# Retention attention ahead of two MLPs on one Trainium2 core: another order of the attention output rows, and the first weight matrix fetched in that order

## The chip, the cores and the metric

The kernel runs on one core of one Trainium2 chip. The metric is the device time of one execution, in microseconds (us), lower is better. The engines of the core are named as in the profile: PE (matmuls), PEld (the loads of a matmul's stationary operand, which overlap PE), DVE, ACT, POOL (element-wise engines) and SP, which here only issues DMAs.

## The reference

What is computed, cut to its core (float32 throughout):

```python
def _attn_ref(q, k, v):            # each (2, 8, 768, 64): batch, heads, tokens, head size
    gamma = 1.0 - 2.0 ** (-5.0 - np.arange(H))          # a decay for each head
    for t in range(S):
        state = gamma[None, :, None, None] * state + einsum('bhd,bhe->bhde', k[:, :, t], v[:, :, t])
        y[:, :, t] = scale * einsum('bhd,bhde->bhe', q[:, :, t], state)

x = attn.transpose(0, 2, 1, 3).reshape(1536, 512)       # feature = head * 64 + e
x = (softplus(x @ moe_w_in)) @ moe_w_out                # 512 -> 2048 -> 512
out = (h * clip(h + 3, 0, 6) / 6) @ moe2_w_out          # h = x @ moe2_w_in, 512 -> 2048 -> 512
```

The weights come as 64-bit floats; the kernel takes them apart itself.

## The kernel before

**Units.** The recurrence is computed in 12 units (2 batches of 6 chunks of 128 tokens), `attend(u)`. A unit has five blocks of matmuls on PE: transposes of k and q (`Tk`, `Tq`), `scores` (S: k against q), `product` (D: k against v, the new state), `carry` (C: the old state against q) and `inner` (I: the masked scores against v). Apart from the transposes, all operands are 64 by 64, a quarter of PE's array: the rows that a matmul uses are the partitions of its operands (0 to 63 or 64 to 127), the columns are the partitions of its output. So there are four **quadrants**, and the program speaks of them through `part[0]` and `part[1]`. A matmul of 64 by 64 in float32 is two MATMUL records in the trace; C, with 16 matmuls, has 32 records. D of a batch's last unit and C of a batch's first unit are half as long.

**Where heads lie.** Head h = 2p + g has its q, k and state on partitions `part[g]` of column block p. Before the change the output of head h is also put on `part[g]` of block p, so that row p * 128 + partition is feature h * 64 + e in the natural order. C therefore goes from rows `part[g]` to columns `part[g]` and uses two of the four quadrants, in turn (L468 to L473). I goes from rows `part[j]` (the two halves of the chunk) to columns `part[g]`, with j innermost, and comes by all four quadrants every two heads (L478 to L483). S and D (all but the short one) use all four in the same way.

**After the matmuls.** DVE makes `pt` from the scores (times the mask, L433); I waits for it. C's output is in one PSUM bank, `oc`; ACT copies it to `oe` (L504); I's output is in two banks, `oi`; DVE adds the two into `on` (L506), and ACT and DVE split that into `x_hi` and `x_lo`, the input of the first MLP.

**MLPs.** All 1536 tokens go in three chunks of 512 through `gemm1` (G1, one bank `h`) and `gemm2` (G2, four banks `acc`, held over 16 steps). Each is twelve matmuls of 128x128 by 128x512 a step. The weights are fetched by `weight(m, o, f)`: 32 pieces of 512 KB for each MLP (16 of the input matrix, o = 0, and 16 of the output matrix), into three slots `raw`, and taken apart by ACT and DVE in some six operations each; the slot is free again after the last of them that reads it. Piece f of an input matrix is one DMA of 128 partitions with four runs of 1 KB on each (L251).

**Order.** `Plan` is a list scheduler that runs while the program is built. Every piece of work is a task with an engine, a cost, a due time and the slots or banks it takes; for each engine the task that can start within a small margin (`NEAR`, 0.5 us on PE) of the earliest and is due first is put next. Due times of PE's tasks are the running sum of the table `cost` (L197). A wait that the plan thinks longer than the margin is filled with another task. `places` gives banks: for one key the bank that came free first, for two keys two **neighbouring** banks (L64 to L67). The first eight units have slots of their own (`hold`), the last four (u = 8 to 11, where tiles appear in the trace as `cv` and `raw`) live in slots that the first weights have left. On the chip each engine takes its instructions in the order of the plan.

Of the kernel before, what the change touches and what calls it, by code (L numbers as in the profile page):

```python
# [13 lines left out]
AF = mybir.ActivationFunctionType  # L14
ALU = mybir.AluOpType
PSUM = bass.MemoryType.PSUM
P = 128
HALF = P // 2
# [101 lines left out]
PSX, TT, TS, ACP, ACS = 0.61, 0.62, 0.36, 0.49, 0.55  # L120
GEMM = 2.73
# [3 lines left out]
def kernel(ctx, tc, q, k, v, w1_in, w1_out, w2_in, w2_out, tq, tk, tcc, out):  # L125
    nc = Plan(tc)
    B, H, S, D = q.shape
    NT, DM = out.shape
    DFF = w1_in.shape[1]
    NP = H // 2  # L130
    KD = DM // P
    NF = DFF // P
    C = P
# [24 lines left out]
    banks = pool("psum", PSUM).tile([P, 8, CH], F32, name="banks")  # L158
# [35 lines left out]


    G = [(m, c, f) for m in range(2) for c in range(NC) for f in range(NF)]
    cost = {"Tk": 0.46, "Tq": 0.46, "S": 0.60, "D": 0.60, "C": 0.98, "I": 0.60, "G1": GEMM, "G2": GEMM}  # L197
    pe = [("Tk", 0), ("Tq", 0)]
    for u in range(START):
        pe += [("S", u), ("D", u)] + ([("Tk", u + 1), ("Tq", u + 1)] if u + 1 < START else []) + [("C", u), ("I", u)]  # L200
# [9 lines left out]
    n = 0  # L210
# [6 lines left out]
    due, t = {}, 5.0  # L217
# [3 lines left out]
    T = {}  # L221
# [7 lines left out]
    def weight(m, o, f, number):  # L229
        key = m, o, f  # L230
        made = conv[0] if m == 0 else []
        use = due[("G2" if o else "G1"), min(m * NC * NF + f, len(G) - LAG)] - 4.0

        def raw():
            return at_slot((f"raw{m}", key))

        def low_word():
            return raw()[:, :, 0]

        def y():  # L240
            return raw()[:, :, 1]

        def w():
            return at_slot((f"cv{m}", key))

        def fetch():
            src = words[m][o]
            if o:
                nc.sync.dma_start(out=raw().rearrange("p n t -> p (n t)"), in_=src[f * P:(f + 1) * P, :])
            else:  # L250
                nc.sync.dma_start(out=raw().rearrange("p (k n) t -> p k (n t)", k=KD),  # L251
                                  in_=src[:, 2 * f * P:2 * (f + 1) * P].rearrange("(k p) f -> p k f", p=P))

        def scale():
            nc.scalar.activation(y().bitcast(F32), y().bitcast(F32), AF.Copy, scale=2.0 ** -112)

        def bits():
            nc.scalar.activation(w(), low_word(), AF.Relu, scale=2.0 ** -29 * (1 - 2.0 ** -12), bias=half)

        def clamp():  # L260
            nc.vector.tensor_scalar(y().bitcast(F32), y().bitcast(F32), -TOP, TOP, ALU.max, ALU.min)

        def sign():
            nc.vector.scalar_tensor_tensor(w(), y(), 0x80000000, w(), ALU.bitwise_and, ALU.bitwise_or)

        def shift():
            nc.vector.scalar_tensor_tensor(w(), y(), 3, w(), ALU.logical_shift_left, ALU.bitwise_or)

        def shifted():
            nc.vector.tensor_scalar(w(), y(), 3, None, ALU.logical_shift_left)  # L270

        def merge():
            nc.vector.scalar_tensor_tensor(w(), low_word(), 29, w(), ALU.logical_shift_right, ALU.bitwise_or)

        def high():
            nc.scalar.activation(w_part(key, 0), w().bitcast(F32), AF.Copy)

        def negative():
            nc.scalar.activation(w_part(key, 1), w().bitcast(F32), AF.Copy, scale=-1.0)

        def low():
            nc.vector.tensor_tensor(w_part(key, 1), w().bitcast(F32), w_part(key, 0).bitcast(F32), ALU.subtract)

        def add():
            nc.gpsimd.dma_start(out=w_part(key, 1).bitcast(F32), in_=w().bitcast(F32), accum_op=ALU.add)

        raw_k, cv_k = (f"raw{m}", key), (f"cv{m}", key)
        cv, part = [(f"cv{m}", cv_k)], [("w", ("w", key))]
        tail = 1.5 if BY_DVE(number) else 7.0
        T["F", key] = t0 = nc.add("SP", 0.45, fetch, due=use - tail - 8.0, take=[(f"raw{m}", raw_k)], load=1.45 if o else 1.75)  # L290
        t1 = nc.add("ACT", 0.57, scale, [t0], use - tail - 3.5)
        t3 = nc.add("DVE", TS, clamp, [t1], use - tail - 2.5)
        if BITS(number):
            t2 = nc.add("ACT", 0.65, bits, [t0], use - tail - 3.0, take=cv)
            t4 = nc.add("DVE", TT, sign, [t3, t2], use - tail - 2.0)
            t5 = nc.add("DVE", TT, shift, [t4], use - tail - 1.3, give=[raw_k])
        else:
            t4 = nc.add("DVE", TS, shifted, [t3], use - tail - 2.4, take=cv)
            t4 = nc.add("DVE", TT, sign, [t4], use - tail - 2.0)
            t5 = nc.add("DVE", TT, merge, [t4], use - tail - 1.3, give=[raw_k])  # L300
        if BY_DVE(number):
            a = nc.add("ACT", ACS, high, [t5], use - 1.5, take=part, give=[cv_k] + made)
            b = nc.add("DVE", TT, low, [a], use - 0.7, give=[cv_k] + made)
        else:
            n = nc.add("ACT", ACS, negative, [t5], use - tail, take=part)
            b = nc.add("POOL", 0.9, add, [n], use - tail + 1, give=[cv_k] + made, load=1.6)
            a = nc.add("ACT", ACS, high, [n], use - 2.5, give=[cv_k] + made)
        T["W", key] = [a, b]
# [49 lines left out]
    def sub(keys, j):  # L358
        i = sorted(nc.slot[x][1] for x in keys)[j]
        return banks[:, i, :NP * HALF].rearrange("p (n t) -> p n t", n=NP)  # L360

    def bank(key):
        return at_slot(key).rearrange("p (n t) -> p n t", n=NP)

    part = [slice(j * HALF, (j + 1) * HALF) for j in range(2)]
    tables, ready = {}, {}

    def attend(u):
        b, i = divmod(u, NCH)
        ph = int(u >= FIRST)  # L370
        d = {n: due.get((n, u)) for n in cost}
        first, last = i == 0, i == NCH - 1
        mine = second if ph else arena

        def task(eng, cost, fn, after, when, take=(), give=(), load=0.0):
            return nc.add(eng, cost, fn, after, when, [(p, k) for p, k in take], list(give) + mine, load)

        def tile_of(n):
            return at_slot((n, u))
# [28 lines left out]
        def turned(n):  # L408
            def go():
                for p in range(NP):  # L410
# [5 lines left out]
                  take=own("kT"), give=[("kP", u)])  # L416
# [7 lines left out]
        sc, ds, oi = ([(n, j, u) for j in range(2)] for n in ("sc", "ds", "oi"))  # L424
# [32 lines left out]
        if not last:  # L457
# [7 lines left out]
            e = task("DVE", 0.42, total, [sm], d["C"] - 0.5, take=[end], give=ds + [mid[1]])  # L465
            ready["end", u] = task("DVE", 0.42, faded, [e, tables["c"]], due["C", u + 1] - 2.0, give=[end[1]])

        def carry():  # L468
            for j in range(int(first), 2):
                w = at_slot(mid[1] if j else ("end", u - 1))  # L470
                for p in range(NP):
                    for g in range(2):
                        nc.tensor.matmul(bank(("oc", u))[part[g], p, part[j]], w[part[g], p, :], tile_of("qT")[part[g], p, part[j]])  # L473

        c = task("PE", cost["C"] / (1 + first), carry, [qt, sm, None if first else ready["end", u - 1]], d["C"],
                 take=[("bank", ("oc", u))], give=[mid[1], ("qT", u)] + ([] if first else [("end", u - 1)]))

        def inner():  # L478
            for h in range(H):
                g, p = h % 2, h // 2  # L480
                for j in range(2):
                    nc.tensor.matmul(sub(oi, j)[part[g], p, :], tile_of("vs")[part[j], h, :], tile_of("pt").rearrange(
                        "p n (g t) -> p g n t", g=2)[part[j], g, p, :])  # L483

        n = task("PE", cost["I"], inner, [pt, vs], d["I"], take=[("bank", x) for x in oi], give=[("pt", u), ("vs", u)])
# [4 lines left out]
        def split(t):  # L490
            return t.rearrange("p n (j t) -> p j n t", j=2)

        def of(n):
            return at_slot((n, u)).rearrange("p (n t) -> p n t", n=NP)

        if first:
            o0 = task("ACT", 0.35, lambda: nc.scalar.activation(split(of("on"))[:, 0], sub(oi, 0), AF.Copy), [n], d["I"] + 0.7,
                      take=[("g", ("on", u))], give=oi)
            o1 = task("ACT", 0.35, lambda: nc.scalar.activation(split(of("oe"))[:, 1], split(bank(("oc", u)))[:, 1], AF.Copy), [c],
                      d["I"], take=[("e", ("oe", u))], give=[("oc", u)])  # L500
            on = task("DVE", 0.42, lambda: nc.vector.tensor_tensor(split(of("on"))[:, 1], split(of("oe"))[:, 1], sub(oi, 1), ALU.add),
                      [n, o0, o1], d["I"] + 1.0, give=oi + [("oe", u)])
        else:
            o1 = task("ACT", ACP, lambda: nc.scalar.activation(of("oe"), bank(("oc", u)), AF.Copy), [c],  # L504
                      d["I"], take=[("e", ("oe", u))], give=[("oc", u)])
            on = task("DVE", PSX, lambda: nc.vector.tensor_tensor(split(of("on")), split(of("oe")), both(oi), ALU.add),  # L506
                      [n, o1], d["I"] + 1.0, take=[("g", ("on", u))], give=oi + [("oe", u)])
        o2 = task("ACT", ACS, lambda: nc.scalar.activation(hi, of("on"), AF.Copy), [on], need - 1.5, give=[("on", u)])
# [147 lines left out]
```

## Time and profile before

| what | us |
|---|---|
| device time, median of 3 runs (607.19 to 609.77) | 607.47 |
| device time of the profiled execution | 606.65 |
| its span, first to last instruction | 604.5 |
| PE busy | 582.9 (96%) |
| DVE busy | 335.9 (56%) |
| ACT busy | 304.7 (50%) |

The span is 2.15 us shorter than the device time of the same execution. Busy shares are means over stages that differ: up to about 128 us the weights of the first MLP are fetched and taken apart, and DVE, ACT and the DMA queues are busier than the shares of the table say; from there on PE works almost without a gap. The mean granted clock of PE is 0.992 of full speed.

### The profile page before, as it was taken

The page shows a single profiled execution, that of the slowest core. Times are in us where ns is not written, and L with a number is a line of the kernel's source. Part 1 is how long each engine was busy: PE and PEld are TensorE (multiplying, and loading weights), DVE is VectorE, ACT ScalarE, POOL GpSimd, SP SyncE. Part 2 cuts the span into 40 slices and gives each one's busy share as a digit, 9 for nine tenths or more (in the row PEclk, how much of TensorE's full clock was granted, in tenths as well). Part 3 has the DMA queues.
Part 4 walks back from the last instruction along what each step waited for, and adds up shares of the span by engine and source line. Part 5 has one row for each costly group of instructions (what it writes and reads, how often), then busy time and mean ns, then how long its engine had stood idle before and what let it go on. Part 6 is the DMA issues. An engine that isn't in the chain of part 4 may idle for free.

```text
span 604.5 us, 9654 instructions
## 1 busy us (share of the span) xinstructions
PE 582.9 (96%) x3891; PEld 478.2 (79%) x3891; DVE 335.9 (56%) x584; ACT 304.7 (50%) x516; POOL 44.3 (7%) x57
## 2 busy tenths in 40 slices
PE   7698889999999999999999999999999999999997
PEld 6576668878788888888888887888888888888886
DVE  4899898995655333376677985622422222322223
ACT  2468877994533333476779996622222222222220
POOL 0001111120000000011122221100000000000000
PEclk9899989999999999999999999999999999999999
DMA  8997776966210100046588987510100000100001
GB/s 193 237 252 199 195 183 158 241 180 137 54 37 21 51 0 1 1 105 157 152 196 212 247 211 176 130 18 0 71 1 1 0 1 0 71 0 1 0 1 69
DMA packets 68364, 59.87 MB, mean 99 GB/s; under 512 B 39776, under 2 KB 56416, under 8 KB 68320
## 3 DMA queue, kind: packets, MB, share of 16 engines
q1 hardware_dynamic: 61264, 46.41, 26.9%
q0 software_dynamic: 7056, 12.85, 12.4%
q8 instruction: 30, 0.49, 0.4%
q14 instruction: 14, 0.11, 0.1%
HBM read 43.26 MB, written 3.15 MB: 77 GB/s over the span
## 4 chain that ended last, share of the span: by engine, by line
PE 76%; DVE 10%; DMA 6%; ACT 5%; issue 3%; SPq 1%; DVEq 0%; ACTq 0%
PE banks L41 76%; DVE cv L41 5%; DMA raw<-in_moe_w_out_dram 3%; DMA raw<-in_moe_w_in_dram 2%; DVE raw L41 1%; ACT w L41 1%; DVE g L41 1%; DVE lo L41 1%; ACT raw L41 1%; DMA v<-in_v_dram 1%; ACT cv L41 1%; ACT e L41 1%; SPq L41 1%; DVE x_lo L41 1%; DVE w L41 1%
## 5 line engine op out<-in xcount | busy, mean ns | idle before, releaser
L41 PE MATMUL banks<-x_hi,w 128*128 128x512 f32 x768 | 254.8, 393 | 5.0 <-ACT kT L41 2.2
L41 PEld LDWEIGHTS banks<-x_hi,w 128*128 128x128 f32 x768 | 144.8, 189 | 37.1 <-DVE g L41 2.5
L41 PE MATMUL banks<-x_lo,w 128*128 128x512 f32 x384 | 150.2, 391 | 0.0
L41 PE MATMUL banks<-hi,w 128*128 128x512 f32 x384 | 127.5, 393 | 0.8 <-ACT w L41 0.5
L41 PE MATMUL banks<-w,hi 128*128 128x512 f32 (+1 forms) x386 | 118.3, 388 | 0.0
L41 DVE SCALAR_TENSOR_TENSOR g<-e,banks 128x512 f32<-128x512 f32 x48 | 33.0, 688 | 114.1 <-ACT e L41 114.0
L41 ACT ACTIVATE e<-banks,three 128x512 f32<-128x512 f32 x48 | 32.9, 686 | 124.6 <-PE banks L41 116.7
L41 DVE SCALAR_TENSOR_TENSOR cv<-raw,cv 128x512 uint32<-128x512 uint32 x128 | 87.5, 689 | 6.7 <-ACT cv L41 4.2
L41 DVE TENSOR_TENSOR lo<-g,hi 128x512 fp32r<-128x512 f32 x96 | 66.2, 690 | 44.7 <-ACT hi L41 43.4
L41 ACT ACTIVATE hi<-g 128x512 fp32r<-128x512 f32 x96 | 60.5, 630 | 49.8 <-DVE g L41 33.3
L41 PEld LDWEIGHTS banks<-hi,w 128*128 128x128 f32 x384 | 72.0, 188 | 17.0 <-ACT w L41 0.9
L41 PEld LDWEIGHTS banks<-x_lo,w 128*128 128x128 f32 x384 | 72.6, 189 | 14.7
L41 PEld LDWEIGHTS banks<-w,hi 128*128 128x128 f32 x386 | 72.4, 188 | 14.9
L41 ACT ACTIVATE w<-cv 128x512 fp32r<-128x512 f32 x113 | 68.3, 624 | 16.7 <-DVE cv L41 16.2
L41 PE MATMUL banks<-lo,w 128*128 128x512 f32 x192 | 75.1, 391 | 1.4 <-DVE lo L41 1.4
L41 PE MATMUL banks<-w,lo 128*128 128x512 f32 (+1 forms) x193 | 74.9, 388 | 0.0
L41 POOL DMA_DIRECT2D w<-cv x49 | 43.3, 887 | 348.9 <-ACT w L41 208.3
L41 ACT ACTIVATE g<-banks 128x512 f32<-128x512 f32 (+1 forms) x50 | 29.2, 584 | 54.7 <-PE banks L41 54.2
L41 ACT ACTIVATE raw<-raw 128x512 f32<-128x512 f32 x64 | 42.7, 667 | 8.7 <-DMA raw<-in_moe_w_out_dram 5.1
L41 PEld LDWEIGHTS banks<-lo,w 128*128 128x128 f32 x192 | 36.0, 188 | 9.5 <-DVE lo L41 2.2
L41 DVE SCALAR_TENSOR_TENSOR g<-g,e 128x512 f32<-128x512 f32 x48 | 33.1, 690 | 16.3 <-ACT e L41 15.7
L41 PEld LDWEIGHTS banks<-w,lo 128*128 128x128 f32 x193 | 36.3, 188 | 7.5
(58 smaller groups left out, 340.2 us busy)
## 6 DMA issues: line engine op xcount, KB each, us to landing
raw<-in_moe_w_in_dram SPq DMA_DIRECT2D x32, 512.0 KB, 4.1
raw<-in_moe_w_out_dram SPq DMA_DIRECT2D x32, 512.0 KB, 4.3
w<-cv POOLq DMA_DIRECT2D x49, 256.0 KB, 4.4
out_dram<-e SPq DMA_DIRECT2D x11, 256.0 KB, 2.0
q<-in_q_dram SPq DMA_DIRECT2D x8, 256.0 KB, 5.0
v<-in_v_dram SPq DMA_DIRECT2D x8, 256.0 KB, 4.9
k<-in_k_dram SPq DMA_DIRECT2D x7, 256.0 KB, 4.7
raw<-in_k_dram SPq DMA_DIRECT2D x4, 256.0 KB, 3.2
```

Source lines behind the costliest of these rows:

```text
L41: return self.plan.tc.keep_in_program_order(getattr(self.engine, op)(*args, **kwargs))
```

## The change

The output of head h goes to the half `h // 4` and block `h % 4`: heads kk and kk + 4 share the rows of block kk. C now goes from rows `part[h % 2]` to columns `part[h // 4]`, so all four quadrants occur in it, and its output is spread over two banks, one for each row half, which must be neighbours. I keeps its order over h and j, and its output half becomes `h // 4`. The ACT copy reads both banks in one instruction, of the same size as before. The rows of the first input matrix must come in the same order: piece f of `moe_w_in` is now fetched by two DMAs, one for partitions 0 to 63 and one for 64 to 127. The plan's cost of C goes from 0.98 to 0.60, that of such a fetch on SP from 0.45 to 0.9.

```diff
-    cost = {"Tk": 0.46, "Tq": 0.46, "S": 0.60, "D": 0.60, "C": 0.98, "I": 0.60, "G1": GEMM, "G2": GEMM}
+    cost = {"Tk": 0.46, "Tq": 0.46, "S": 0.60, "D": 0.60, "C": 0.60, "I": 0.60, "G1": GEMM, "G2": GEMM}
...
-            else:
+            elif m:
                 nc.sync.dma_start(out=raw().rearrange("p (k n) t -> p k (n t)", k=KD),
                                   in_=src[:, 2 * f * P:2 * (f + 1) * P].rearrange("(k p) f -> p k f", p=P))
+            else:
+                for g in range(2):
+                    nc.sync.dma_start(out=raw()[g * HALF:(g + 1) * HALF].rearrange("p (k n) t -> p k (n t)", k=KD),
+                                      in_=src[g * KD * HALF:(g + 1) * KD * HALF, 2 * f * P:2 * (f + 1) * P].rearrange("(k p) f -> p k f", p=HALF))
...
-        T["F", key] = t0 = nc.add("SP", 0.45, fetch, ..., load=1.45 if o else 1.75)
+        T["F", key] = t0 = nc.add("SP", 0.45 if o or m else 0.9, fetch, ..., load=1.45 if o else 1.75)
...
+        oc = [("oc", x, u) for x in range(2)]
+
+        def crossed():
+            a, b = sorted(nc.slot[x][1] for x in oc)
+            return banks[:, a:b + 1:b - a, :NP * HALF].rearrange("p x (n t) -> p x n t", n=NP // 2)
+
         def carry():
             for j in range(int(first), 2):
                 w = at_slot(mid[1] if j else ("end", u - 1))
-                for p in range(NP):
-                    for g in range(2):
-                        nc.tensor.matmul(bank(("oc", u))[part[g], p, part[j]], w[part[g], p, :], tile_of("qT")[part[g], p, part[j]])
+                for h in range(H):
+                    g, p = h % 2, h // 2
+                    nc.tensor.matmul(crossed()[part[h // NP], g, p % 2, part[j]], w[part[g], p, :], tile_of("qT")[part[g], p, part[j]])

         c = task("PE", cost["C"] / (1 + first), carry, [qt, sm, None if first else ready["end", u - 1]], d["C"],
-                 take=[("bank", ("oc", u))], give=[...])
+                 take=[("bank", x) for x in oc], give=[...])

         def inner():
             for h in range(H):
                 g, p = h % 2, h // 2
                 for j in range(2):
-                    nc.tensor.matmul(sub(oi, j)[part[g], p, :], ...)
+                    nc.tensor.matmul(sub(oi, j)[part[h // NP], h % NP, :], ...)
...
+        late = slice(HALF if first else 0, C)
+        o1 = task("ACT", 0.35 if first else ACP, lambda: nc.scalar.activation(
+            of("oe").rearrange("p (n x) t -> p x n t", x=2)[:, :, :, late], crossed()[:, :, :, late], AF.Copy), [c],
+            d["I"], take=[("e", ("oe", u))], give=oc)
...
-            o1 = task("ACT", ACP, lambda: nc.scalar.activation(of("oe"), bank(("oc", u)), AF.Copy), [c],
-                      d["I"], take=[("e", ("oe", u))], give=[("oc", u)])
```

## Rows read from the trace of the kernel before

**Rows 1.** The page: busy time of each engine over the span.

```profile
PE 582.9 (96%) x3891; PEld 478.2 (79%) x3891; DVE 335.9 (56%) x584; ACT 304.7 (50%) x516; POOL 44.3 (7%) x57
```

**Rows 2.** Stretches: length, busy us of each engine (instructions), PE clock, DMA share, GB/s.

```profile
10.00:20.00 10.00, 8.71 (x278) 7.20 (x278) 8.60 (x17) 3.77 (x7) 0.00 (x0) 1.00 1.01 263
20.00:30.00 10.00, 5.83 (x156) 5.20 (x156) 8.96 (x18) 5.86 (x10) 0.00 (x0) 0.74 0.97 202
...
50.00:90.00 40.00, 33.36 (x325) 25.44 (x324) 37.18 (x70) 33.08 (x59) 6.17 (x7) 0.96 0.76 195
...
140.00:205.00 65.00, 64.99 (x742) 52.88 (x740) 34.67 (x61) 25.54 (x44) 0.00 (x0) 1.00 0.25 58
...
500.00:550.00 50.00, 50.00 (x222) 41.40 (x222) 15.23 (x23) 12.58 (x19) 0.00 (x0) 1.00 0.06 22
```

**Rows 3.** The chain that ended last, in order of time: start, length, what.

```profile
12.77 7.34 DMA raw<-in_moe_w_in_dram
...
105.02 3.85 DMA raw<-in_moe_w_in_dram
...
128.54 23.43 PE banks L41 x106
```

**Rows 4.** Waits up to 150 us: engine and tile, releaser, total us, times, longest.

```profile
ACT raw L41 <- DMA raw<-in_moe_w_in_dram: 3.5, 3, 1.8
```

**Rows 5.** Timeline of PE, unit 9 (D, then S, C, I): start, length, instruction, count.

```profile
168.96 0.39 PE L41 MATMUL banks<-hi,w 128*128 128x512 f32 x1
169.28 0.69 PE L41 MATMUL banks<-cv,raw 64*64 64x64 f32 x32
...
170.24 0.39 PE L41 MATMUL banks<-x_lo,w 128*128 128x512 f32 x1
...
172.54 0.39 PE L41 MATMUL banks<-x_hi,w 128*128 128x512 f32 x1
172.85 0.69 PE L41 MATMUL banks<-cv,raw 64*64 64x64 f32 x32
173.37 1.11 PE L41 MATMUL banks<-cv,st 64*64 64x64 f32 x32
174.36 0.69 PE L41 MATMUL banks<-cv,cv 64*64 64x64 f32 x32
...
175.32 0.40 PE L41 MATMUL banks<-lo,w 128*128 128x512 f32 x1
```

**Rows 6.** Timeline of DVE beside it: the multiplication that makes pt.

```profile
173.62 0.69 DVE L41 TENSOR_TENSOR cv<-banks,small 128x512 f32<-128x512 f32 x1 [1.70 <-PE banks L41]
```

**Rows 7.** Timeline of PE, unit 8: C (cv,st) and I (cv,cv) between matmuls of the MLP.

```profile
158.14 0.39 PE L41 MATMUL banks<-x_hi,w 128*128 128x512 f32 x1
158.45 1.08 PE L41 MATMUL banks<-cv,st 64*64 64x64 f32 x29
159.32 0.27 PE L41 MATMUL banks<-cv,cv 64*64 64x64 f32 x1
159.33 0.22 PE L41 MATMUL banks<-cv,st 64*64 64x64 f32 x1
...
159.38 0.22 PE L41 MATMUL banks<-cv,st 64*64 64x64 f32 x2
159.43 0.64 PE L41 MATMUL banks<-cv,cv 64*64 64x64 f32 x30
...
160.34 0.39 PE L41 MATMUL banks<-lo,w 128*128 128x512 f32 x1
```

**Rows 8.** Groups of instructions by tile: C's matmul records, count, duration ns min/median/max.

```profile
L41 PE MATMUL banks<-cv,st x128: 218/218/267, 158.5 to 204.3; 64*64 64x64 f32 x128
```

**Rows 9.** Stretches in which fetches of an input matrix land (columns as in rows 2).

```profile
17.50:19.75 2.25, 1.49 (x39) 1.11 (x30) 2.11 (x5) 0.63 (x1) 0.00 (x0) 1.00 1.07 367
```

**Rows 10.** Timeline of SP's DMA issues: start, time to issue, what, count.

```profile
12.77 2.33 SPq L41 DMA_DIRECT2D raw<-in_moe_w_in_dram  x3
...
15.77 4.57 SPq L41 DMA_DIRECT2D k<-in_k_dram  x1
```

More of the change, by code (lines that the diff above doesn't have):

```diff
@@ L289, in weight @@
         tail = 1.5 if BY_DVE(number) else 7.0
-        T["F", key] = t0 = nc.add("SP", 0.45, fetch, due=use - tail - 8.0, take=[(f"raw{m}", raw_k)], load=1.45 if o else 1.75)
+        T["F", key] = t0 = nc.add("SP", 0.45 if o or m else 0.9, fetch, due=use - tail - 8.0, take=[(f"raw{m}", raw_k)], load=1.45 if o else 1.75)
         t1 = nc.add("ACT", 0.57, scale, [t0], use - tail - 3.5)
@@ L470, in carry @@
                 w = at_slot(mid[1] if j else ("end", u - 1))
-                for p in range(NP):
-                    for g in range(2):
-                        nc.tensor.matmul(bank(("oc", u))[part[g], p, part[j]], w[part[g], p, :], tile_of("qT")[part[g], p, part[j]])
+                for h in range(H):
+                    g, p = h % 2, h // 2
+                    nc.tensor.matmul(crossed()[part[h // NP], g, p % 2, part[j]], w[part[g], p, :], tile_of("qT")[part[g], p, part[j]])
         c = task("PE", cost["C"] / (1 + first), carry, [qt, sm, None if first else ready["end", u - 1]], d["C"],
-                 take=[("bank", ("oc", u))], give=[mid[1], ("qT", u)] + ([] if first else [("end", u - 1)]))
+                 take=[("bank", x) for x in oc], give=[mid[1], ("qT", u)] + ([] if first else [("end", u - 1)]))
         def inner():
@@ L481, in inner @@
                 for j in range(2):
-                    nc.tensor.matmul(sub(oi, j)[part[g], p, :], tile_of("vs")[part[j], h, :], tile_of("pt").rearrange(
+                    nc.tensor.matmul(sub(oi, j)[part[h // NP], h % NP, :], tile_of("vs")[part[j], h, :], tile_of("pt").rearrange(
                         "p n (g t) -> p g n t", g=2)[part[j], g, p, :])
@@ L498, in attend @@
                       take=[("g", ("on", u))], give=oi)
-            o1 = task("ACT", 0.35, lambda: nc.scalar.activation(split(of("oe"))[:, 1], split(bank(("oc", u)))[:, 1], AF.Copy), [c],
-                      d["I"], take=[("e", ("oe", u))], give=[("oc", u)])
             on = task("DVE", 0.42, lambda: nc.vector.tensor_tensor(split(of("on"))[:, 1], split(of("oe"))[:, 1], sub(oi, 1), ALU.add),
@@ L503, in attend @@
         else:
-            o1 = task("ACT", ACP, lambda: nc.scalar.activation(of("oe"), bank(("oc", u)), AF.Copy), [c],
-                      d["I"], take=[("e", ("oe", u))], give=[("oc", u)])
             on = task("DVE", PSX, lambda: nc.vector.tensor_tensor(split(of("on")), split(of("oe")), both(oi), ALU.add),
```

## The prediction

> **What bounds the kernel now.** I read the busy shares first [rows 1]: PE works 582.9 of 604.5 us, so only some 22 us of the span are not matmuls. The stretches then show where [rows 2]. From 140 us on PE has no gap (64.99 of 65, 50.00 of 50): there a shorter matmul block is gained in full. Between 50 and 90 us PE idles 6.6 of 40 us while DVE is busy 37.2: there PE waits for weights, and what PE saves becomes a longer wait. In the opening, 10 to 30 us, the DMA engines are full (share 1.01 and 0.97) and DVE has little left (8.6 and 9.0 of 10). The chain of waits agrees [rows 3]: it begins in the opening with the first fetch of the input matrix (7.34 us), passes through another (3.85 us at 105 us), and is PE alone only from 128.5 us. So two prices are needed: PE's time in units 8 to 11, after 140 us, and whatever delays the weights before.
>
> **C and I.** A 64x64 record lasts 0.218 us [rows 8], but records on different quadrants overlap. C of unit 9 has 32 records on two quadrants, so 16 steps; its last starts 15 steps after its first: (1.11 - 0.22) / 15 = 0.059 us a step [rows 5]. S, D and I, on four quadrants, need 8 steps, 0.47 us, which fits their 0.69 us from first start to last end. How far does PE look ahead for a free quadrant? Unit 8 shows it [rows 7]: two matmuls of I start at 159.32 and .33, a step before the last two of C (159.38), on the quadrants that C doesn't use, though I's first matmul in the program goes to a quadrant that C still holds. As two of I and not more do so, and only one step ahead, I take it that a quadrant holds one matmul waiting behind the one at work, and that a third blocks all that follow.
>
> By that, with a and b for the row halves in front of the first column half, c and d for the second: new C is issued as ab ab cd cd, twice. The second pair waits, the third finds its quadrants free: 8 steps instead of 16, **-0.47 us**. New I is issued as ab four times, then cd four times. c and d can only begin when the third ab starts, 4 steps late: 12 steps instead of 8, **+0.24 us**. The change spreads C over four quadrants and takes that order from I.
>
> [...]
>
> **Where the gain goes in units 8 to 11.** A block alone between matmuls of the MLP also costs a change-over. For D of unit 9: 170.24 - 168.96 = 1.28 us, less two regular matmuls at 50.00 / 222 = 0.225 us, less 8 steps: 0.36 us [rows 2, 5]. S, C and I of unit 9 stand in one line: 175.32 - 172.54 - 0.45 = 2.33 us. I starts at 174.36; `pt`, for which it waits, is ready at 173.62 + 0.69 = 174.31 [rows 6]. Today C just covers that wait: in one line, a C that ends 0.47 us earlier only waits for `pt`, and the longer I makes it 2.57.
>
> But the line is unlikely to stay. C now takes two neighbouring banks. S holds two, `acc` four, and G1 needs one for `h`: eight banks don't hold all. So C will mostly come after `pt` has given S's banks back, and I after ACT's copy has given C's back; the plan fills waits over 0.5 us with a step of the MLP, as it does between S and C of unit 8. Three blocks alone cost (8 + 8 + 12) x 0.059 + 3 x 0.36 = 2.73 us: +0.40 for units 9, 10 and 11 each. Unit 8 has S alone now, 0.83, and C with I 160.34 - 158.14 - 0.45 = 1.75 [rows 7], 2.58 in all: +0.15. Upper end +1.35 us. Lower end: C and I together and I still 8 steps, 0.83 + 16 x 0.059 + 0.36 = 2.13, which gives 3 x -0.20 - 0.45 = -1.05 us. I take **+0.9**, near the upper end for the banks. The ACT copy reads the same 512 columns in one instruction: nothing, and PE doesn't wait for ACT there.
>
> Units 0 to 7 have the same blocks before 128 us, where the weights pace PE: 0, at best 6 x -0.23 = -1.4 us (in the two units with half a C, gain and loss are equal). The plan's due times move up by 0.38 us a unit, which may reorder tasks on any engine; no row prices that, and I leave it inside the range.
>
> **The split fetch.** 16 fetches become 32. SP issues one more each; in the opening an issue takes 2.33 / 3 = 0.78 us, but the next one stands 4.57 us, since the queue is full [rows 10], so the issue hides behind transfers. It costs up to 0.78 us a piece if that cover is gone. The two halves have the same 512 runs of 1 KB. While such fetches land, 367 GB/s move [rows 9]: 512 KB in 1.43 us. No DMA of 64 partitions to a 512 KB tile is in the trace. If both halves move together, the price is 0. If the rate goes with the partitions, each half takes as long as the whole did: +1.43 us. Nothing in the rows decides; I take the middle, 0.7 us.
> In the opening three fetches stand ahead of k of unit 3, which is needed before the first G1: 3 x 0.7 = **+2.1 us** (0 to 4.3), since DMA is full and the chain starts here. Behind them in SP's queue stand v and k of unit 3 and all of units 4 to 7, and T, D and S wait for them. Of the 13 later fetches most are hidden by the three slots: up to 150 us ACT waited only 3 times for this kind [rows 4]. Two or so arrive late: **+1.0 us** (0 to 13 x 1.43 / 3 = 6.2, if all three slots always turn on it).
>
> Sum: 0.9 + 2.1 + 1.0 = +4.0 us. Against the profiled execution, 606.65 (2.15 more than its span), that is 610.65; the median of the runs is 0.82 above that execution, so 611.5.
>
> **Rivals.**
> 1. The halves overlap (not slower). If the second half's transfer begins with the first and both move at the whole's rate, the fetch costs nothing, and +0.9 is left: 608.4, or 606.4 at the lower end of C and I. It decides below about 0.47 us a fetch, where 0.9 + 3 x 0.47 + 1.0 x 0.47 / 0.7 comes to +3.0. For it: the full queue, and the same runs of 1 KB. Against: a full DMA queue in the opening has no cover for a slower half.
> 2. Each half at half rate, one after the other: 4.3 in the opening, 2 x 1.43 = 2.9 at the two awaited later, and 0.9: +8.1, so 615.6. For it: DMA share 1.01, and a chain that begins there.
> [...]
> 3. Faster: PE paces the first 128 us too, and I keeps its 8 steps. Then 11 units' worth of C count (two of 12 are halves): 11 x 0.47 = 5.2 us, 602.3. Against: 6.6 us idle between 50 and 90.
> 4. The change doesn't do what it says: the first heads' ab ab holds C at two quadrants. Then C keeps 16 steps: 4 x 0.47 = 1.9 more than the forecast, 613.4. Against: rows 7.
>
> **How the numbers follow.** A measurement of this kernel tells about 0.5%, 3.0 us, from no change: 604.4 to 610.5 is "same". Forecast 0.42 (611.5, own range 609 to 615, a quarter of it under 610.5), rival 1 0.30 (nearly all same), rival 2 0.14, rival 3 0.09, rival 4 0.05. Slower: 0.31 + 0.13 + 0.04 = 0.48; same: 0.11 + 0.29 and the rest of the others, 0.43; faster 0.09. The range leaves out rival 3 and the upper half of rival 2: 605.5 to 616.
>
> **What would show it.** C: 32 records in about 0.7 us from first start to last end, with four at a time; I: about 0.92. If I stays at 0.69, the look-ahead is deeper than I took it. S, C and I apart, with MLP matmuls between, in units 9 to 11. The first fetch lands over 0.5 us later than 20.1 us, and PE becomes gapless some 3 us later than 128.5; if it does so at the same time, the split fetch was free and rival 1 is right. If the time falls by over 3 us, I was wrong that weights pace the first part.

## The result, and the profile after

| | us, median (range) | profiled execution | its span |
|---|---|---|---|
| before | 607.35 (607.12 to 609.77) | 606.65 | 604.5 |
| changed | 612.48 (611.03 to 614.91) | 613.58 | 611.8 |

The changed kernel takes 1.0079 times the time of before, 95% interval 1.0052 to 1.0106: slower by 4.8 us, where the sum of the prediction said 4.0. The total was right. What it was put together from was not, and that is what the experiments are about. The two profiled executions lie 6.9 us apart and the medians 5.1, so nearly 2 us of what the two traces show is the spread between executions.

The page of the changed kernel: busy time of the engines, and the queue that carries SP's DMAs (packets, MB, share of 16 engines over the span).

```profile
PE 584.4 (96%) x3891; PEld 476.5 (78%) x3891; DVE 336.2 (55%) x584; ACT 304.9 (50%) x516; POOL 44.5 (7%) x57
q1 hardware_dynamic: 61520, 46.41, 28.6%
```

The same line of the queue on the page of before:

```profile
q1 hardware_dynamic: 61264, 46.41, 26.9%
```

PE's busy time rose by 1.5 us only [rows 1], so the span's 7.3 us are mostly waiting. The queue moved the same 46.41 MB, but its packets took 0.286 x 611.8 = 175.0 us of all 16 engines, not 0.269 x 604.5 = 162.6. The 12.4 us are 0.77 us for each of the 16 fetches that are split, if they are put down to these alone. Where the waiting lies is seen in the stretches of the changed kernel (columns as in rows 2):

```profile
10.00:20.00 10.00, 9.46 (x321) 7.89 (x320) 8.76 (x18) 3.76 (x7) 0.00 (x0) 1.00 1.08 216
20.00:30.00 10.00, 3.46 (x94) 3.02 (x92) 7.97 (x17) 6.05 (x10) 0.00 (x0) 0.66 1.06 206
50.00:90.00 40.00, 32.12 (x323) 25.67 (x314) 35.12 (x64) 31.34 (x56) 6.59 (x7) 0.91 0.86 196
140.00:205.00 65.00, 63.23 (x642) 49.56 (x641) 38.92 (x70) 30.26 (x53) 0.86 (x1) 1.00 0.30 66
500.00:550.00 50.00, 50.00 (x222) 41.39 (x222) 15.00 (x22) 11.89 (x18) 0.00 (x0) 1.00 0.06 21
```

From 500 us on nothing differs. Between 10 and 20 us the DMA engines are full before and after (shares 1.01 and 1.08), but they move 216 GB/s for 263. Between 50 and 90 the share is 0.86 for 0.76 at the same 195 GB/s. As busy or busier DMA engines for no more bytes is what to see here. It holds over the traces of the experiments below: between 10 and 20 us the five traces with the first matrix split by partitions show 209 to 218 GB/s, the eight with one DMA a piece 242 to 263; between 50 and 90 us the shares are 0.77 to 0.86 and 0.68 to 0.77. The chain of waits of the changed kernel (start, length, what):

```profile
19.18 7.42 DMA k<-in_k_dram
...
34.65 8.00 DMA raw<-in_moe_w_in_dram
...
47.04 8.24 DMA raw<-in_moe_w_in_dram
...
110.87 6.28 DMA raw<-in_moe_w_in_dram
...
130.94 5.50 DMA raw<-in_moe_w_in_dram
```

Before, the input matrix stood in it twice [rows 3], now four times, up to 136 us. In a second trace of the changed kernel (its repeat below) it stands there only twice. ACT's waits for that matrix up to 150 us (total, times, longest) went from 3.5 us in 3 [rows 4] to:

```profile
ACT raw L41 <- DMA raw<-in_moe_w_in_dram: 10.6, 11, 2.2
```

The second trace, of an execution of 609.05 us where this one took 613.58, has half of that:

```profile
ACT raw L41 <- DMA raw<-in_moe_w_in_dram: 5.3, 5, 2.9
```

In the five split traces these waits are 5 to 11, of 5.3 to 12.0 us together, and in the eight with whole fetches 3 or 4, of 1.6 to 3.6 us.

SP's issues in the opening (start, time to issue, what), against rows 10: three whole fetches took 2.33 us, six halves take 5.42, and `k` goes out 3.4 us later.

```profile
13.02 5.42 SPq L41 DMA_DIRECT2D raw<-in_moe_w_in_dram  x6
18.53 0.55 SPq L41 DMA_DIRECT2D v<-in_v_dram  x1
19.18 1.71 SPq L41 DMA_DIRECT2D k<-in_k_dram  x1
```

Last, PE's timeline of the changed kernel: C (cv,st) and I (cv,cv) of unit 8, then S (cv,raw) and C, I of unit 9.

```profile
164.75 0.39 PE L41 MATMUL banks<-x_hi,w 128*128 128x512 f32 x1
165.07 0.68 PE L41 MATMUL banks<-cv,st 64*64 64x64 f32 x30
...
165.64 0.87 PE L41 MATMUL banks<-cv,cv 64*64 64x64 f32 x30
166.44 0.50 PE L41 MATMUL banks<-hi,w 128*128 128x512 f32 x1
166.77 0.39 PE L41 MATMUL banks<-lo,w 128*128 128x512 f32 x1
...
176.27 0.39 PE L41 MATMUL banks<-hi,w 128*128 128x512 f32 x1
176.59 0.69 PE L41 MATMUL banks<-cv,raw 64*64 64x64 f32 x32
177.21 0.50 PE L41 MATMUL banks<-x_hi,w 128*128 128x512 f32 x1
177.55 0.39 PE L41 MATMUL banks<-x_lo,w 128*128 128x512 f32 x1
...
179.84 0.39 PE L41 MATMUL banks<-x_hi,w 128*128 128x512 f32 x1
180.16 0.74 PE L41 MATMUL banks<-cv,st 64*64 64x64 f32 x32
180.92 0.97 PE L41 MATMUL banks<-cv,cv 64*64 64x64 f32 x32
181.82 0.50 PE L41 MATMUL banks<-hi,w 128*128 128x512 f32 x1
182.16 0.39 PE L41 MATMUL banks<-lo,w 128*128 128x512 f32 x1
```

C's block went from 1.11 to 0.74 us and I's from 0.69 to 0.97 [rows 5]. S now stands alone, with steps of the MLP behind it; C and I stayed in one line. Between C and I stands a short wait. ACT's timeline beside it has the copy of the MLP's bank `h` (g) and then the copy of C's two banks (e):

```profile
180.27 0.60 ACT L41 ACTIVATE g<-banks 128x512 f32<-128x512 f32 x1 [3.10 <-PE banks L41]
180.95 0.60 ACT L41 ACTIVATE e<-banks 128x512 f32<-128x512 f32 x1
```

### The profile page after: what moved, and what is told of

The parts are those of the page before. It is cut to its first block, busy times and chain, and to the rows that moved or that the text cites. A ratio compares the mean times of both kernels' runs of the same rounds, so it can differ in the third digit from the quotient of the medians.

```text
span 611.8 us, 9701 instructions
## 1 busy us (share of the span) xinstructions
PE 584.4 (96%) x3891; PEld 476.5 (78%) x3891; DVE 336.2 (55%) x584; ACT 304.9 (50%) x516; POOL 44.5 (7%) x57
## 3 DMA queue, kind: packets, MB, share of 16 engines
q1 hardware_dynamic: 61520, 46.41, 28.6%
q0 software_dynamic: 7056, 12.85, 12.4%
## 4 chain that ended last, share of the span: by engine, by line
PE 77%; DMA 9%; DVE 7%; ACT 5%; issue 2%; SPq 0%; POOL 0%; DVEq 0%; ACTq 0%; POOLq 0%
PE banks L41 77%; DMA raw<-in_moe_w_in_dram 5%; DMA raw<-in_moe_w_out_dram 3%; DVE cv L41 3%; ACT w L41 1%; DMA k<-in_k_dram 1%; ACT raw L41 1%; DVE lo L41 1%; ACT g L41 1%; DVE g L41 1%; ACT cv L41 1%; ACT e L41 1%; DVE x_lo L41 1%; DVE raw L41 0%; ACT hi L41 0%
## 5 line engine op out<-in xcount | busy, mean ns | idle before, releaser
L41 PE MATMUL banks<-hi,w 128*128 128x512 f32 x384 | 129.4, 399 | 7.2 <-DVE g L41 6.3
L41 ACT ACTIVATE raw<-raw 128x512 f32<-128x512 f32 x64 | 42.8, 668 | 16.8 <-DMA raw<-in_moe_w_in_dram 10.6
```

The lines of the kernel that those rows point to most:

```text
L41: return self.plan.tc.keep_in_program_order(getattr(self.engine, op)(*args, **kwargs))
```

## The experiments

Three questions: what does the split cost, and is it the second DMA or the half of the partitions; what do the new numbers in the plan do; what do the new places of C and I do. Ratios are to before, measured beside each run. The runs were on several chips, so kernels of different experiments are compared by their ratios and not by their times.

### The whole fetch in the new order

```diff
-            elif m:
+            elif True:      # the fetch of one DMA, rows in the old order
```

> The changed kernel in its own order of instructions on every engine, but each piece of the first input matrix is fetched whole again, by one DMA of 128 partitions (its rows then come in the old order, so the first MLP multiplies them with the wrong features; time alone is read). Theory A, the split fetch delays the weights: of the 5.1 us between the medians (607.35 and 612.48) some 4 go, 608 to 609, and what stays is the matmul blocks' +1.0 us. Theory B, the plan delays them (C now waits for two neighbouring banks, unit 7 ends some 11 us later and gives up its slots later): 611.5 to 612.5, no change.

604.09 us, ratio 0.9955 (0.9924 to 0.9986). The split costs 1.0079 - 0.9955 = 0.0124, or 7.5 us, and what is left of the change is faster than before, which I had not expected of either theory. ACT's waits for the input matrix, in the changed kernel 10.6 us in 11, are here:

```profile
ACT raw L41 <- DMA raw<-in_moe_w_in_dram: 2.1, 3, 1.5
```

### The split fetch in the old kernel

```diff
+            else:           # first matrix: two DMAs of 64 partitions, rows in the old order
+                for g in range(2):
+                    gs = slice(g * HALF, (g + 1) * HALF)
+                    nc.sync.dma_start(out=raw()[gs]..., in_=src[...][gs])
```

> The kernel before, with the split fetch of the first input matrix alone: one DMA for partitions 0 to 63 and one for 64 to 127, natural row order, the plan's costs untouched, so every engine has the order of before. Theory A: 3 to 5 us slower than before, 610.4 to 612.4. Theory B: 607.4 to 608.

614.26 us, ratio 1.0117 (1.0079 to 1.0154): 7.1 us from the split alone, theory A in kind and more than its 3 to 5. The waits are back where nothing but the fetch was changed:

```profile
ACT raw L41 <- DMA raw<-in_moe_w_in_dram: 8.5, 9, 1.8
```

### Two DMAs over all partitions

```diff
-                    nc.sync.dma_start(out=raw()[g * HALF:(g + 1) * HALF]...)
+                    ks = slice(g * KD // 2, (g + 1) * KD // 2)
+                    nc.sync.dma_start(out=raw()...[:, ks], in_=src[...][:, ks])   # 128 partitions, two blocks of rows
```

> The changed kernel, each piece of the first input matrix in two DMAs again, but cut by blocks instead of partitions: two of the four blocks on all 128 partitions each (rows in the old order, time alone is read). If half the partitions are what costs: as with the whole fetch, 608 to 609. If a second DMA to issue and to wait for is what costs: as the changed kernel, 612.5.

606.86 us, ratio 0.9998 (0.9973 to 1.0022). As many DMAs of as many bytes as in the changed kernel, and 0.0081 or 4.9 us less: most of the price is the half of the partitions. The second DMA costs the 0.0043 or 2.6 us to the whole fetch, but the intervals of these two ratios overlap. The DMA groups between 12 and 150 us (count, KB each, us from issue to landing), first of this kernel, then of the changed one:

```profile
raw<-in_moe_w_in_dram SPq DMA_DIRECT2D x32, 256.0 KB, 4.2
```

```profile
raw<-in_moe_w_in_dram SPq DMA_DIRECT2D x32, 256.0 KB, 5.5
```

The packets say the same. Time of a 1 KB packet in ns between 50 and 150 us of the span, from the DMA records (mean; 10, 50 and 90%):

```
before                      54   46  46  46
changed                     72   46  74  93
whole fetch, new order      55   46  46  46
split by partitions, old    68   46  67  91
two DMAs of 128 partitions  51   46  46  60
```

### Split only the second MLP's matrix

```diff
-            else:
+            elif not m:
+                (whole)
+            else:
+                (two DMAs of 64 partitions)
```

> The kernel before, with the fetches of the second MLP's input matrix (255 to 350 us, where PE is never without work) split into two DMAs of 64 partitions. A measure of the transfer by itself: today a piece of that stretch lands 3.4 to 3.9 us after its issue. If both halves move together: the same. If each half moves at half the rate: about 1.4 us more from the first issue to the last landing. Time 607.4 either way, since nothing waits there.

608.88 us, ratio 1.004 (1.001 to 1.0069). My cover was not complete: of the profiled execution's 4.1 us of delay 2.1 arise between 332 and 370 us, where both matrices are fetched together. The other 2.0 arise before 121 us, where nothing differs from before: so far apart are two executions of the same opening. But this kernel shows the price of a half by itself, since seven fetches stand alone there. Landings between 257 and 298 us, of before and of this kernel:

```profile
raw<-in_moe_w_in_dram SPq DMA_DIRECT2D x7, 512.0 KB, 3.8
```

```profile
raw<-in_moe_w_in_dram SPq DMA_DIRECT2D x14, 256.0 KB, 4.0
```

A half takes no less than the whole. Issue by issue, a pair takes 4.9 us from its first issue to its last landing (median of the seven), the whole 3.8: 1.1 us more, between the nothing of halves that move together and the 1.4 expected of halves at half the rate. The second half is issued 0.64 us behind the first and lands 1.2 us behind it.

### Only the plan's numbers

```diff
-    cost = {..., "C": 0.98, ...}
+    cost = {..., "C": 0.60, ...}
-        ... nc.add("SP", 0.45, fetch, ...)
+        ... nc.add("SP", 0.45 if o or m else 0.9, fetch, ...)
```

> Before, with nothing changed but two numbers that the plan reckons with: C 0.60 for 0.98, and 0.90 of SP's time for an issue of the first matrix. The work, the layout, the banks and the DMAs are those of before. The planner then sets S, D, C and I of units 4 to 7 in other gaps between the MLP steps. Theory A (the gain of about 3 us that the whole fetch in the new order showed comes from the order that the changed costs give): 603.5 to 605.5, and a first stretch (to the MLP step of unit 8) shorter by 2 to 4 us. Theory B (it comes from C itself, its two banks or its four quadrants, in the first 128 us): 607 to 609. Theory C (an order laid out for a shorter C than the true one loses what the order gains): above 609.

604.57 us, ratio 0.9959 (0.9932 to 0.9985), with the layout and the DMAs of before. Theory A by its time: the order of tasks that the new numbers give is worth about 2.5 us, though C lasts as long as it did. Its other sign, a first stretch shorter by 2 to 4 us, isn't in the trace, whose execution took 606.04 us: the MLP step of unit 8 starts at 148.01 us, before at 148.28. So where the gain lies isn't shown. This kernel computes all of the reference and is the fastest of those here that do.

### C's number alone

```diff
-    cost = {..., "C": 0.98, ...}
+    cost = {..., "C": 0.60, ...}
```

> Before with one number changed: C 0.60 for 0.98 in the plan, SP's 0.45 kept. With both numbers the time was 604.6. If C's number makes the order that gains, 603.5 to 605.5 again; if SP's number does, 607 to 608.5.

605.69 us, ratio 0.9978 (0.9954 to 1.0002). Outside both expectations, between them; it doesn't tell how the gain divides between the two numbers.

### The new order with the old numbers

```diff
 (the whole fetch in the new order, and)
-    cost = {..., "C": 0.60, ...}      SP 0.9
+    cost = {..., "C": 0.98, ...}      SP 0.45
```

> The changed kernel with the whole fetch (rows in the old order), and the plan's costs as before: C 0.98, 0.45 of SP's time for an issue. C in two banks and four quadrants, I in two, are kept. It leaves out the order of the weight's rows, so the output is not the reference's. Theory A (the gain is the plan's): it is lost, 607 to 609, that is before plus about 0.8 from the 4 x 0.24 of I's steps and the waits in units 8 to 11. Theory B (the gain is C's own): 603.5 to 605.

605.90 us, ratio 0.9977 (0.9947 to 1.0007): below theory A's figures, above theory B's. It is 0.0022 above the same kernel with the new numbers.

### The changed kernel with the old numbers, and itself again

```diff
-    cost = {..., "C": 0.60, ...}      SP 0.9
+    cost = {..., "C": 0.98, ...}      SP 0.45
```

> The changed kernel with C at 0.98 and 0.45 of SP's time for an issue in the plan, as before: split fetch, new rows, C in four quadrants, I in two. Theory A (the plan's order gives its 2 to 3 us whether the first matrix is split or not): 613 to 616, that is 2 to 3 above the changed kernel beside it. Theory B (with the split fetch the weights pace the opening so wholly that the order no longer matters): within 1 us of the changed kernel.

612.97 us, ratio 1.0095 (1.0068 to 1.0123).

> The changed kernel itself, beside three variants of it on one chip. The one with I's heads in the other order took 609.2, of which its pace in units 8 to 11 explains 1.05 us; its first 140 us were shorter by another 5 although no order differs. Theory A (that is the spread of the opening from execution to execution, or from chip to chip): the changed kernel takes 610 to 612 here. Theory B (I's longer block costs more than its steps): 612.5 or more.

610.29 us, ratio 1.0057 (1.0034 to 1.0079): theory A of the second, and with 2.7 us between the two, theory A of the first. The changed kernel's two measurements, 1.0079 and 1.0057, differ by as much as some of the effects looked for; below I use their mean, 1.0068. Their traces differ more: where unit 8 begins the second is 4.4 us ahead.

These runs make a table of ratios, each part of the change with and without the others:

```
                          whole fetch    split fetch    the split costs
old layout, old numbers   1              1.0117         0.0117
old layout, new numbers   0.9959         -
new layout, old numbers   0.9977         1.0095         0.0118
new layout, new numbers   0.9955         1.0068         0.0113
```

The split costs the same three times, 0.0116 or **7.0 us**. The numbers give 0.0041, 0.0022 and 0.0027, on average 0.0030 or **-1.8 us**; in the last two pairs the intervals of the two ratios overlap. The layout gives 0.0023, 0.0022 and 0.0004, on average 0.0016 or **-1.0 us**, which with intervals of about 0.003 on each ratio isn't told from nothing. Their sum is +4.2 us.

### I in four quadrants

```diff
-            for h in range(H):
+            for h in (0, 4, 1, 5, 2, 6, 3, 7):      # in I alone
```

> The changed kernel with I's heads issued in the order 0, 4, 1, 5, 2, 6, 3, 7, so that four matmuls in a row go to four quadrants. All engines' orders and the fetches stay as in the changed kernel. By the step of 0.059 us I starts its 16 matmuls over 8 steps and not 12, its block goes from 0.97 back to about 0.73 us, and the four units that stand in a row of paced matmuls give back about 4 x 0.24 = 1 us: 611 to 612 against 612.5 of the changed kernel. If the 12 steps aren't what makes I longer, the block stays at 0.97 us and the time at 612.5.

609.22 us, ratio 1.0026 (0.9995 to 1.0056): 2.6 us under the mean of the changed kernel, where the steps explain 1. The rest is about what the changed kernel's own two measurements differ by (0.0022, or 1.3 us).

> The changed kernel with the whole fetch and with I's heads issued so that they use four quadrants: what the change of layout could reach if the rows cost nothing. It leaves out the order of the weight's rows, so the output is not the reference's. The whole fetch alone gave 604.1; I back to 8 steps gives 4 x 0.24 us in units 8 to 11: 602.5 to 604. Before with the plan's costs alone took 604.6: if C's four quadrants gave something of their own in the first 128 us, this one is faster than that by over 1 us; if not, by at most 0.5, since C's four units in the paced part give 4 x 0.47 us less what the two bank waits cost.

602.36 us, ratio 0.9930 (0.9902 to 0.9957): 1.5 us under the whole fetch alone, and 1.8 under the plan's numbers alone, which by that expectation speaks for a gain of C's own in the first 128 us; the intervals of the two overlap, so it stays a hint. PE's timeline of this kernel, C and I of unit 9:

```profile
168.09 0.39 PE L41 MATMUL banks<-x_hi,w 128*128 128x512 f32 x1
168.41 0.74 PE L41 MATMUL banks<-cv,st 64*64 64x64 f32 x32
169.17 0.69 PE L41 MATMUL banks<-cv,cv 64*64 64x64 f32 x32
169.79 0.50 PE L41 MATMUL banks<-hi,w 128*128 128x512 f32 x1
170.13 0.39 PE L41 MATMUL banks<-lo,w 128*128 128x512 f32 x1
```

I is back at 0.69 us: nothing but the order in which its heads are issued made it 0.97. The starts of some steps of the MLP (of their first weight load, us from the span's start) show what that is worth where PE is paced by its own work (G1 number 17 to number 25, in which units 8 to 11 lie), and how the opening differs (G1 number 0):

```
                             G1 0    G1 17    G1 25    17 to 25
before                       33.91   148.28   207.68   59.40
changed                      34.78   154.98   215.19   60.21
changed, again               35.59   150.57   210.78   60.21
whole fetch, new order       32.74   146.04   206.24   60.20
split fetch, old kernel      35.62   154.07   213.43   59.36
whole, new, old numbers      32.70   145.73   206.01   60.28
changed, old numbers         35.32   154.73   215.01   60.28
changed, I four quadrants    35.02   149.66   208.78   59.12
whole, I four quadrants      32.72   143.47   202.58   59.11
pairs in q and k             36.51   151.40   210.45   59.05
two DMAs of 128, new order   34.00   146.68   206.89   60.21
split of the second MLP      35.56   150.31   209.71   59.40
plan's numbers alone         33.05   148.01   207.29   59.28
C's number alone             35.98   151.01   210.30   59.29
```

The last column repeats to 0.1 us wherever units 8 to 11 are the same. The first two don't: the second MLP's split has the opening of before, and stands 1.65 us later at G1 0.

### Pairs made where q and k are loaded

```diff
-   heads 2p and 2p + 1 share a tile of q, k and the state; first matrix split
+   heads p and p + 4 share it: q and k come by two DMAs each, of four heads and 128 partitions; C writes part[p % 2];
+   output rows in the order of the matrix, which is fetched whole; D issues heads 0, 4, 1, 5, 2, 6, 3, 7, I issues 0 to 7 and writes part[h % 2];
+   SP's number in the plan 0.45, as before
```

> A version that takes the gains without the split of the first matrix: heads kk and kk + 4 are paired where q and k are loaded (two DMAs over all 128 partitions for each of them, four heads each), so that transposes, state and C work on such pairs, C goes to four quadrants of two banks, and the output rows come out in the order of the weight's rows. The first matrix is fetched whole, D and I issue their heads so that they use four quadrants, C's cost in the plan is 0.60. The whole fetch in the new order took 604.1. I back to 8 steps gives up to 1 us more; 31 more DMAs of q and k at 0.6 us of SP's time cost between 0 and 2 us, in the first 60 us above all. Expected: 602.5 to 605.5, faster than both kernels.

608.26 us, ratio 0.9999 (0.9968 to 1.0031). Not faster: the first MLP step starts at 36.51 us, 3.8 later than with the whole fetch in the new order, and the delay stays to G1 25 (+4.2). The cost of the rows' order was moved from the weights to q and k, in the same full opening; that its DMAs cause the 3.8 us is argued, not shown, and C's number alone, with none of these DMAs, came to 35.98 in its trace.

## Why the prediction was right in sum and wrong in its terms

**The opening.** +2.1 us was predicted. Split against whole, G1 0 starts 2.0 us later (changed), 1.7 (old kernel) and 2.6 (old numbers): 2.1 on average. The `k` that SP issues behind the three fetches lands at 26.60 us where the whole fetch in the new order has it at 24.46, again 2.1, and in the second trace of the changed kernel 1.9. So the price and its place are right, to within what single executions tell. In the new layout the two groups stand apart, 34.78 to 35.59 in four split traces and 32.70 to 32.74 in three whole ones; in the old layout the whole fetch alone gives 33.05 to 35.98, which covers the split kernel's 35.62.

**The later fetches: the step that failed.** I wrote that of the 13 later fetches most are hidden by the three slots, that two or so arrive late, +1.0 us. The runs leave 7.0 less 2.1, **+4.9 us**. The traces of the new layout agree: at G1 17 the three split ones are on average 7.5 us behind the two whole ones, at G1 0 2.5. The price of one was not the main error: 0.77 us more of all DMA engines a fetch stands beside the 0.7 that I took, and a pair that stands alone lands 1.1 us later. The number exposed was. I read rows 4, three waits, as cover for the rest, but a count of waits that exist doesn't say how far the others are from waiting. Rows 2 hinted at it: DMA share 0.76 and PE 6.6 us idle between 50 and 90 us, so that much of that stretch hangs on the weights, and in the split kernels ACT waited 5 to 11 times. By these prices 4.9 us are 4 to 6 of 13 fetches, not 1.4; that count is worked out, not seen. My upper bound of 6.2 held it; my value within it was too near the lower end.

**The mechanism of the split.** Rival 2, each half as long as the whole, serial, has 4.3 + 2.9 = 7.2 us for the split, almost the 7.0 measured, but its terms are not: the opening cost half of its 4.3 and the later fetches more than its 2.9. It was called 615.6 because it had nothing on the other side. Rival 1, halves that cost nothing together, fell with the 7.0 us and with the 1.1 of a pair that stands alone. What a pair costs lies between the two rivals. Packets of the split kernel last 74 ns in the middle and 93 where the slowest tenth begins, against 46 before: 1.6 and 2.0 times. Half rate, as rival 2 has it, would be 2 throughout; why the middle one lies below it isn't shown. I had given rival 2 a chance of 0.14.

**The plan.** "No row prices that, and I leave it inside the range", with the value 0. It was -1.8 us, and -2.5 with everything else untouched. With the layout's first eight units, also taken at 0, it hid most of the error above. That is why the sum came out, and that is luck: +2.1 and +0.8 as predicted, +4.9 for the later fetches in place of +1.0, and some -3.6 for the plan's order and the first eight units (-1.8, and -1.0 - 0.8, of which the -1.0 isn't told from nothing).

**Units 8 to 11.** +0.9 predicted; G1 17 to 25 takes 60.21 for 59.40: **+0.8**. Not by the path described, though: S does stand alone, but C and I stayed in one line. S alone is 177.55 - 176.27 - 0.45 = 0.83, C with I 182.16 - 179.84 - 0.45 = 1.87, in which I starts 0.23 us after C's last start. It waits there for a bank, but not for one of C's: ACT's copy of C's banks begins at 180.95 us, after the block I did (180.92). What released it, at 180.87, is the end of ACT's copy of the MLP's bank `h`. Together 2.70 against 2.33 before; three separate blocks had been worked out as 2.73. Unit 8 came out the other way: C with I 166.77 - 164.75 - 0.45 = 1.57 for 1.75, so -0.18 where I had +0.15. -0.18 + 3 x 0.37 = +0.9.

**C and I.** Right in kind, a step off in size. S, on four quadrants, has 0.69 - 0.22 = 0.47 us between first and last start, 8 steps of 0.059. C has 0.74 - 0.22 = 0.52, **9 steps**, and I 0.97 - 0.22 = 0.75, **13**. I had said 8 and 12. The starts of the single records in unit 9 speak for the look-ahead. C's first records on the second column half start 0.03 us after its first, and I's 0.29 us after, with the fifth start on the first half, as one waiting matmul for each quadrant has it. What I had left out is that in S, C and I of unit 9 the first record on each quadrant lasts 0.267 us and not 0.218, the two lengths of [rows 8]. S pays that once; with it its 7 intervals between 8 starts come to 0.47 us, which I had read as 8 steps. I pays it twice, one after the other: that is its 13th step. C's 9th, a few hundredths lost at the turn to the other half, stays unexplained. With I's heads issued over four quadrants the stretch G1 17 to 25 falls to 59.1: the 1.1 us are what the order of I costs in four units. Rival 4, C at 16 steps, fell.

**Rival 3** (602.3, PE paces the first part and I keeps its steps) needed a split for nothing. Where the fetch is whole and I has four quadrants, the time is 602.36, but part of that is the plan's.

**What stays open.** How the plan's 1.8 us divide over its tasks: single executions of one kernel differ by up to 4.4 us before unit 8. How much of the split's 7.0 us lies in the opening, to better than 1 us, for the same reason. In the changed kernel the granted clock between 20 and 30 us was 0.66 of full speed in one trace (0.5 for 6.8 us, else 1.0), with PE busy for 3.5 us, and 0.88 in the other, with 5.2; what that costs isn't told apart from the waits. And whether C's quadrants gain anything before 128 us: the layout's -1.0 us is inside its interval.

## What to carry over

This layout saved matmul steps and was paid for where its order is made, in the DMA: halves of 64 partitions cost 7.0 us, two DMAs over all 128 some 2.6, not clearly told from nothing. So cost such a DMA by its partitions, or move the order to a place where the DMA engines aren't full, as they are in the opening (shares 1.01 and 1.08). Read how many transfers are exposed from the stretches (is an engine waiting for that stream at all), not from the count of waits that already show. And when a planner's numbers change with the kernel, run the numbers alone first: here they were worth about 2 us, while the layout that they came with couldn't be told from nothing.

## What was not expected of the hardware

- A DMA of 64 partitions and 256 KB lands in 4.0 us where one of 128 partitions and 512 KB lands in 3.8 (second MLP, fetches that stand alone). Between 50 and 150 us, among other fetches, the middle 1 KB packet lasts 74 ns in the kernel with such halves, against 46.
- The same bytes in two DMAs over all 128 partitions keep the 46 ns, and cost some 2.6 us in all, not clearly told from nothing.
- Sixteen 64x64 matmuls issued as four pairs on one half of the columns and four on the other take 13 steps of 0.059 us, and 8 when four in a row go to four quadrants: 0.97 and 0.69 us for the same work.
